# Attention and token mixer on one core: weight rows in contiguous eights, row-tiled transposes, and a transfer order from a queue model

## The chip, the cores and the metric

One core of one Trainium2 chip. The metric is device time in microseconds (us) of one execution; a profile's span is some 1.8 us shorter, since it runs from the first to the last instruction. TensorE (PE; its weight loads are PEld), VectorE (DVE), ScalarE (ACT), GpSimd (POOL) and SyncE (SP, which issues most DMAs) run side by side. "Clock" is the mean share of TensorE's full clock that the throttle granted.

## The reference

```python
scores = scale * (q @ k^T)          # 8 batches, 16 query heads over 4 key heads, 384 tokens, head 64
x = softmax(scores) @ v             # put together to [8, 384, 1024]
wq, wk = x @ w_q, x @ w_k           # both [1024, 64]
mixed = (scale * wq @ wk^T) @ x     # token mixing, no softmax
out = relu(mixed) @ w_out           # [1024, 1024]
```

Inputs and output are float32; the kernel computes in bf16 with float32 accumulation.

## The kernel before

The program is one long static list of instructions. A small scheduler in the generator keeps a clock for each engine, books a duration for every step and picks the next step for TensorE; its guesses fix the order, not the times on the chip. Four PSUM banks are shared by everything that is not a score. The parts that matter:

```python
def attend(b, g, u):                      # 12 matmuls of 65 columns, then the normalisation
    ...                                   # cut: ps = one of four banks
    nc.vector.reciprocal(out=rcp, in_=avv[:, :, D])
    nc.vector.tensor_tensor(out=xnats[b][:, c, h0:h0 + G, :], in0=avv[:, :, :D],
                            in1=rcp.to_broadcast([P, G, D]), op=ALU.mult)
    bank_free[at] = on("dve", 665, pe(370))      # what the scheduler books for it

def x_tr(b, c):                           # x transposed on TensorE: 8 blocks of 128x128 into one bank
    for dc in range(DC):
        nc.tensor.transpose(out=ps[:, dc, :], in_=xn[:, c, dc * P:(dc + 1) * P], identity=ident)
    nc.vector.tensor_copy(out=xTs[b][:, :, c, :], in_=ps)

def x_by_dma(b, c):                       # other chunks of x are transposed by DMA
    return b > 0 and c < C - 1
...                                       # cut: order of the first transfers
load(0); load(1)                          # k, q, v of batches 0 and 1
# w_q, w_k, then w_out: row c*128 + p on partition p
nc.sync.dma_start(out=wld[:, dc:dc + 2, :],
                  in_=moe_w_out[dc * P:(dc + 2) * P, :].rearrange("(c p) n -> p c n", p=P))
# load(2) follows when batch 1's scores begin, so behind w_out in the queue
```

`keep_busy` issues dummy matmuls (on a tile `idle`) where the scheduler sees TensorE wait, meant to hold its clock up (in the profile before, after 2.87 us without a matmul, the granted clock was 0.50 from 45 to 50 us).

The softmax here doesn't subtract the row's maximum and nothing guards it: scores larger than these inputs give would overflow.

Of the kernel before, what the change touches and what calls it, by code (L numbers as in the profile page):

```python
# [15 lines left out]
def kernel(  # L16
# [17 lines left out]

    nc = tc.nc
# [14 lines left out]
    NWIDE = 0  # L50
    NB = 4
    NPT = 9
    EAGER = 1
    DMA_TR = 5500
# [24 lines left out]
    clk = {"pe": 0.0, "dve": 0.0, "act": 0.0}  # L79
    mode = ["full"]  # L80
    wide_ps = [psG.tile([P, 2, NH], F32, name=f"wide{i}") for i in range(NWIDE)]
    bank_ps = [psG.tile([P, NH], F32, name=f"bank{i}") for i in range(NB)]
    wide_free = [0.0] * NWIDE
# [16 lines left out]

    def when(*keys):
        return max(ready.get(key, INF) for key in keys)
# [4 lines left out]

    def wide():
        return min((f, i) for i, f in enumerate(wide_free))
# [12 lines left out]
    def load(b):  # L122
        kraw = raw_p.tile([P, Hkv, C, D], F32, name="kraw")
        vraw = raw_p.tile([P, Hkv, C, D], F32, name="vraw")
        qraw = raw_p.tile([P, Hq, C, D], F32, name="qraw")
        raws[b] = (kraw, vraw, qraw)

        def ld(dst, src, a, z, c0=0, c1=C):
            nc.sync.dma_start(out=dst[:, a:z, c0:c1],  # L129
                              in_=src[b, a:z].rearrange("h (p c) d -> p h c d", p=P)[:, :, c0:c1])  # L130

        half = Hq // KP
        if b == 0:
            ld(kraw, k, 0, 2)
            ld(qraw, q, 0, half, 0, 1)
            ld(qraw, q, 0, half, 1, C)
            ld(vraw, v, 0, 2)
            ld(kraw, k, 2, 4)
            ld(qraw, q, half, Hq)
            ld(vraw, v, 2, 4)  # L140
        else:
            ld(kraw, k, 0, 4)
            ld(qraw, q, 0, half)
            ld(qraw, q, half, Hq)
            ld(vraw, v, 0, 4)
# [5 lines left out]
    def cast_k(b, kp, eng):  # L151
        for u in range(2):
            eng.tensor_copy(out=nats[b][0][:, kp, :, u, :], in_=raws[b][0][:, 2 * kp + u])  # L153

    def cast_q(b, kp, eng):
        for u in range(2):
            h0 = (2 * kp + u) * G
            eng.tensor_copy(out=nats[b][1][:, :, kp, :, u, :].rearrange("p c i d -> p i c d"),  # L158
                            in_=raws[b][2][:, h0:h0 + G])

# [4 lines left out]
    def cast_v(b, kp, eng):  # L165
        eng.tensor_copy(out=vexts[b % 3][:, 2 * kp:2 * kp + 2, :, :D],
                        in_=raws[b][1][:, 2 * kp:2 * kp + 2])

# [17 lines left out]
    def tr_dma(b, part):  # L186
        kb, qb = nats[b]
        KT, QT = trs[b]
        if part == 0:
            nc.sync.dma_start_transpose(out=KT, in_=kb.rearrange("p a c u d -> p (a c u d)"))  # L190
            for kp in range(KP):
                ready["K", b, kp] = clk["pe"] + DMA_TR
        else:
            c, n = part - 1, KP * G
            nc.sync.dma_start_transpose(out=QT[:, c * n:(c + 1) * n, :],
                                        in_=qb[:, c].rearrange("p a i u d -> p (a i u d)"))
            for kp in range(KP):
                ready["Q", b, kp, c] = clk["pe"] + DMA_TR

    def tr_k(b, kp0, kp1):  # L200
        kb, _ = nats[b]
        KT, _ = trs[b]
        _, i = bank()
        ps = bank_ps[i].bitcast(BF16).rearrange("p (n t) -> p n t", n=8)
        n = 0
        for kp in range(kp0, kp1):
            for c in range(C):
                nc.tensor.transpose(out=ps[:, n, :], in_=kb[:, kp, c].rearrange("p u d -> p (u d)"),
                                    identity=ident)
                n += 1  # L210
        nc.vector.tensor_copy(out=KT[:, kp0 * C:kp1 * C, :], in_=ps[:, :n, :])
        done = bank_free[i] = on("dve", 360 if n == C else 560, pe(56 * n))
# [3 lines left out]
    def tr_q(b, blocks):  # L216
# [3 lines left out]
        _, i = bank()  # L220
        ps = bank_ps[i].bitcast(BF16).rearrange("p (n t) -> p n t", n=8)
        for n, (c, kp) in enumerate(blocks):
            for j in range(G):
                nc.tensor.transpose(out=ps[:, n * G + j, :],
                                    in_=qb[:, c, kp, j].rearrange("p u d -> p (u d)"), identity=ident)
        end = pe(56 * G * len(blocks))
        if len(blocks) == 2 and blocks[1][0] == blocks[0][0]:
            t0 = (blocks[0][0] * KP + blocks[0][1]) * G
            nc.vector.tensor_copy(out=QT[:, t0:t0 + 2 * G, :], in_=ps)
            done = on("dve", 690, end)  # L230
        else:
            for n, (c, kp) in enumerate(blocks):
                t0 = (c * KP + kp) * G
                nc.vector.tensor_copy(out=QT[:, t0:t0 + G, :], in_=ps[:, n * G:(n + 1) * G, :])
                done = on("dve", 420, end)
        bank_free[i] = done
# [34 lines left out]
    def attend(b, g, u):  # L271
# [3 lines left out]
        if g == 0 and u == 0:  # L275
            xnats[b] = x_p.tile([P, C, Hq, D], BF16, name="xnat", bufs=3)
# [3 lines left out]
        for i in range(G):  # L280
            for kc in range(C):
# [7 lines left out]
        nc.vector.tensor_tensor(out=xnats[b][:, c, h0:h0 + G, :], in0=avv[:, :, :D],  # L289
                                in1=rcp.to_broadcast([P, G, D]), op=ALU.mult)  # L290
# [9 lines left out]
    def x_by_dma(b, c):  # L300
        return b > 0 and c < C - 1
# [8 lines left out]
    def x_tr_dma(b, c):  # L310
        x_open(b)
        xn = xnats[b].rearrange("p c h d -> p c (h d)")
        nc.sync.dma_start_transpose(out=xTs[b][:, :, c, :], in_=xn[:, c, :])
        ready["T", b, c] = when(("X", b, c, 0), ("X", b, c, 1)) + DMA_TR

    def x_tr(b, c):
        x_open(b)
        xn = xnats[b].rearrange("p c h d -> p c (h d)")
        _, i = bank()
        ps = bank_ps[i].bitcast(BF16).rearrange("p (n t) -> p n t", n=DC)  # L320
        for dc in range(DC):
            nc.tensor.transpose(out=ps[:, dc, :], in_=xn[:, c, dc * P:(dc + 1) * P], identity=ident)  # L322
        nc.vector.tensor_copy(out=xTs[b][:, :, c, :], in_=ps)  # L323
        ready["T", b, c] = bank_free[i] = on("dve", 690, pe(450))
# [19 lines left out]
    def wk_tr(b):  # L344
        wT, _ = wqs[b]
        _, i = bank()
        ps = bank_ps[i].bitcast(BF16).rearrange("p (n t) -> p n t", n=8)
        for c in range(C):
            nc.tensor.transpose(out=ps[:, c, :], in_=wT[:, c * P:(c + 1) * P], identity=ident)  # L349
        wkN = small_p.tile([P, C, Dh], BF16, name="wkN")  # L350
        nc.vector.tensor_copy(out=wkN, in_=ps[:, :C, Dh:2 * Dh])
        wkNs[b] = wkN
        ready["N", b] = bank_free[i] = on("dve", 250, pe(165))

    def mix_c(b):
        wkN = wkNs[b]
        xn = xnats[b].rearrange("p c h d -> p c (h d)")
# [37 lines left out]
    def po():  # L395
# [29 lines left out]
        if half == 1 and not last:  # L425
            nc.sync.dma_start(out=dst, in_=osb)

# [5 lines left out]
    def after_s(b, s):  # L433

        n = b + 1
        if b == 0 or n >= B:
            return
        if s == 0:
            load(n)
        elif s == 5:  # L440
            cast(n)
            start_tr(n)
        elif s in (9, 11, 13, 15):
            tr_dma(n, (s - 9) // 2)
# [17 lines left out]

    def cand_a():
# [3 lines left out]
        return max(when(*[("P", b, C * g + kc) for kc in range(C)]), ready["V", b], bank()[0])  # L467
# [12 lines left out]
    def chain_open(b):  # L480
        todo = []
        for c in range(C):
            if not x_by_dma(b, c):
                todo.append((lambda c=c: when(("X", b, c, 0), ("X", b, c, 1)), lambda c=c: x_tr(b, c), 1))
        todo.append((lambda: max(when(*[("T", b, c) for c in range(C)]), ready["Wt"]), lambda: wqk(b), 1))
        todo.append((lambda: when(("W", b)), lambda: wk_tr(b), 1))
# [13 lines left out]
    def cand_po():  # L500
# [4 lines left out]
        if i is None:  # L505
            t = max(t, when(("M", b, DCS[-1])), bank()[0])
        return t

    def step():
# [15 lines left out]
        for b in sorted(chains):  # L525
# [5 lines left out]
            if todo[0][-1] == "tiled" and pair is not None and pair < now + 1200:  # L531
# [8 lines left out]
        if not cands:  # L540
            return False
        ok = [x for x in cands if x[0] <= now]
# [4 lines left out]
        if go is None:  # L547
# [3 lines left out]
            for b in sorted(chains):  # L551
                todo = chains[b]
                if todo and todo[0][-1] == "tiled" and cand_chain(b) <= clk["pe"] + 20:
                    todo.pop(0)[1]()
                    break
# [3 lines left out]

# [9 lines left out]
    nc.sync.dma_start(out=wqkld[:, :, 0, :], in_=moe_w_q.rearrange("(c p) h -> p c h", p=P))  # L569
    nc.sync.dma_start(out=wqkld[:, :, 1, :], in_=moe_w_k.rearrange("(c p) h -> p c h", p=P))  # L570
    wld = wld_p.tile([P, DC, Dm], F32, name="wld")
    for dc in range(0, DC, 2):
        nc.sync.dma_start(out=wld[:, dc:dc + 2, :],
                          in_=moe_w_out[dc * P:(dc + 2) * P, :].rearrange("(c p) n -> p c n", p=P))
# [5 lines left out]
    clk["pe"] = clk["dve"] = clk["act"] = 4000.0  # L580
    tr_k(0, 0, 1)
    cast_qc(0, 0, 0, 0, nc.vector.tensor_copy)
    cast_qc(0, 0, 0, 1, nc.scalar.copy)
    keep_busy(900)
    clk["pe"] = clk["dve"] = 5200.0
# [11 lines left out]
    nc.gpsimd.tensor_copy(out=wqk_sb[:, :, Dh:], in_=wqkld[:, :, 1, :])  # L597
    for dc in range(DC):
        nc.gpsimd.tensor_copy(out=wout_sb[:, dc, :], in_=wld[:, dc, :])  # L599

    for b in range(B):
        ready["V", b] = 0.0
    ready["V", 0] = 11000.0
    ready["Wt"], ready["Wo"] = 24000.0, 30000.0
    prep += [
        (lambda: 8600.0, lambda: tr_q(0, [(1, 0), (2, 0)])),
        (lambda: 12500.0, lambda: tr_k(0, 1, 2)),
        (lambda: 13500.0, lambda: tr_q(0, [(0, 1), (1, 1)])),
        (lambda: 13500.0, lambda: tr_q(0, [(2, 1)])),
        (lambda: 21000.0, lambda: tr_k(1, 0, 2)),  # L610
        (lambda: 22000.0, lambda: tr_q(1, [(0, 0), (0, 1)])),
        (lambda: 22000.0, lambda: tr_q(1, [(1, 0), (1, 1)])),
        (lambda: 22000.0, lambda: tr_q(1, [(2, 0), (2, 1)])),
    ]
    prep = [(lambda at=at: max(at(), bank()[0]), lambda go=go: (prep.pop(0), go())) for at, go in prep]
# [33 lines left out]
```

## Time and profile before

| | before |
|---|---|
| time, at first | 224.09 us median of 3 (223.12 to 225.83) |
| TensorE busy | 95% of a span of 224.3 us |
| VectorE / ScalarE busy | 65% / 63% |
| x normalisation (L289) | 96 x 425 ns |
| the profiled execution | 226.12 us, clock 0.985, slower than every timed run (the record marks its state as slow) |

The prediction below shows the lines that carry this. How to read them: TensorE is at work nearly all the time and after about 50 us never waits, so the end is set by how much TensorE work is left then; a group's "idle before" names what its engine waited for, and its mean is the length of one record, not the pace (L322's transposes are 220 ns long and start 56 ns apart).

### The profile page before, as it was taken

How to read it: one execution, taken by the hardware profiler on the slowest of the kernel's cores; microseconds unless marked ns; L12 is line 12 of the kernel's file. 1: busy time of each engine (PE TensorE's matmuls, PEld its weight loads, DVE VectorE, ACT ScalarE, POOL GpSimd, SP SyncE). 2: the span in 40 equal slices, each digit the busy share in tenths (PEclk: the TensorE clock that was granted, in tenths of full speed). 3: DMA queues.
4: the chain of work that ended last, by engine and by line, in shares of the span. 5: the costliest groups of instructions: out<-in, count | busy, mean ns of one | idle time of the engine just before them, and what ended most of it. 6: DMA issues, size and time to landing. Idle time of an engine off the chain costs nothing.

```text
span 224.3 us, 5470 instructions
## 1 busy us (share of the span) xinstructions
PE 214.2 (95%) x2217; PEld 113.6 (51%) x2244; DVE 145.2 (65%) x365; ACT 140.6 (63%) x146; POOL 52.1 (23%) x97
## 2 busy tenths in 40 slices
PE   8999999589999999999999999999999999999993
PEld 5666665245545545454555546554555553434441
DVE  2355786834697758865887648874679569576332
ACT  3599998747788778887887887887888600000000
POOL 1385678406300540045016100620000000000000
PEclk9999999959999999999999999999999999999999
DMA  6996999999399979999999998989224422242424
GB/s 174 324 327 170 410 386 325 136 237 323 65 183 215 335 166 187 222 338 216 223 229 342 154 213 260 281 205 154 99 91 53 143 93 93 93 190 93 180 101 187
DMA packets 71688, 46.09 MB, mean 205 GB/s; under 512 B 42736, under 2 KB 67568, under 8 KB 71664
## 3 DMA queue, kind: packets, MB, share of 16 engines
q1 hardware_dynamic: 71520, 45.62, 77.6%
q8 instruction: 17, 0.28, 0.5%
q10 hardware_dynamic: 144, 0.13, 0.2%
q14 instruction: 7, 0.06, 0.1%
HBM read 23.59 MB, written 12.58 MB: 161 GB/s over the span
## 4 chain that ended last, share of the span: by engine, by line
PE 74%; DMA 14%; DVE 3%; SPq 3%; POOL 3%; issue 1%; DVEq 0%
PE bank L408 37%; PE bank L282 13%; PE sc L259 12%; DMA qraw<-in_q_dram 12%; PE bank L331 4%; SPq L129 3%; PE bank L384 3%; PE bank L362 2%; DMA QT<-qb 2%; PE bank L322 1%; POOL qb L158 1%; DVE osb L421 1%; PE bank L349 1%; DVE msb L389 1%; POOL wqk_sb L596 1%
## 5 line engine op out<-in xcount | busy, mean ns | idle before, releaser
L263 ACT ACTIVATE pt<-sc 128x1024 bf16<-128x1024 f32 x144 | 138.9, 1023 | 34.6 <-PE sc L259 34.4
L408 PE MATMUL bank<-wout_sb,msb 128*128 128x512 bf16 x357 | 91.7, 382 | 1.3 <-issue 0.5
L408 PEld LDWEIGHTS <-msb 128*128 128x128 bf16 x384 | 33.8, 98 | 42.4 <-issue 13.7
L259 PE MATMUL sc<-QT,KT 64*128 64x512 bf16 x288 | 47.5, 387 | 3.1 <-DMA QT<-qb 2.9
L282 PEld LDWEIGHTS <-pt 128*128 128x128 bf16 x1152 | 41.9, 98 | 15.8 <-issue 9.9
L282 PE MATMUL bank<-vext,pt 128*128 128x65 bf16 x1152 | 46.9, 195 | 0.4 <-DVE osb L421 0.2
L421 DVE COPY osb<-bank 128x512 f32<-128x512 f32 (+1 forms) x49 | 33.1, 677 | 21.7 <-PE bank L408 20.5
L289 DVE TENSOR_TENSOR xnat<-bank,rcp 128x256 bf16<-128x256 f32 x96 | 40.8, 425 | 3.3
L389 DVE TENSOR_SCALAR msb<-bank 128x384 bf16<-128x384 f32 x64 | 32.5, 551 | 9.5 <-PE bank L384 9.0
L287 DVE RECIPROCAL rcp<-bank 128x4 f32<-128x4 f32 x96 | 16.9, 176 | 17.6 <-PE bank L282 16.7
L158 POOL CAST qb<-qraw 128x768 bf16<-128x768 f32 x30 | 24.0, 827 | 17.4 <-DMA qraw<-in_q_dram 15.1
L153 POOL CAST kb<-kraw 128x192 bf16<-128x192 f32 x30 | 9.2, 347 | 67.3 <-DMA kraw<-in_k_dram 67.3
L259 PEld LDWEIGHTS <-KT 64*128 64x128 bf16 x288 | 12.4, 94 | 24.1 <-issue 17.2
L117 PE MATMUL bank<-idle 128*128 128x256 bf16 x80 | 14.8, 324 | 1.0 <-DVE idle L562 1.0
L331 PE MATMUL bank<-xT,wqk_sb 128*128 128x384 bf16 x64 | 11.7, 327 | 0.0
L117 PEld LDWEIGHTS <-idle 128*128 128x128 bf16 x80 | 7.9, 114 | 6.6 <-issue 4.0
L384 PE MATMUL bank<-wT,Csb 64*128 64x384 bf16 x32 | 10.6, 332 | 0.4 <-DVE rcp L287 0.3
L384 PE MATMUL bank<-wq,Csb 64*128 64x384 bf16 x32 | 10.6, 332 | 0.0
L599 POOL CAST wout_sb<-wld 128x1024 bf16<-128x1024 f32 x8 | 8.1, 1040 | 4.1 <-DMA wld<-in_moe_w_out_dram 4.1
L366 DVE CAST Csb<-bank 128x512 bf16<-128x512 f32 x8 | 5.5, 688 | 5.2 <-PE bank L362 5.2
L337 DVE CAST wT<-bank 128x384 bf16<-128x384 f32 x8 | 4.5, 558 | 6.7 <-PE bank L331 6.7
L323 DVE COPY xT<-bank 128x1024 bf16<-128x1024 bf16 x10 | 6.9, 688 | 2.5 <-PE bank L322 2.5
(33 smaller groups left out, 70.1 us busy)
## 6 DMA issues: line engine op xcount, KB each, us to landing
out_dram<-osb SPq DMA_DIRECT2D x23, 512.0 KB, 3.1
qraw<-in_q_dram SPq DMA_DIRECT2D x15, 768.0 KB, 7.4
wld<-in_moe_w_out_dram SPq DMA_DIRECT2D x4, 1024.0 KB, 9.5
kraw<-in_k_dram SPq DMA_DIRECT2D x7, 384.0 KB, 4.3
vraw<-in_v_dram SPq DMA_DIRECT2D x7, 384.0 KB, 8.9
qraw<-in_q_dram SPq DMA_DIRECT2D x1, 512.0 KB, 5.3
kraw<-in_k_dram SPq DMA_DIRECT2D x2, 192.0 KB, 3.7
vraw<-in_v_dram SPq DMA_DIRECT2D x2, 192.0 KB, 6.3
```

Source lines behind the costliest of these rows:

```text
L117: nc.tensor.matmul(out=bank_ps[i][:, :256], lhsT=idle[:, :P], rhs=idle, start=True, stop=True)
L158: eng.tensor_copy(out=nats[b][1][:, :, kp, :, u, :].rearrange("p c i d -> p i c d"), in_=raws[b][2][:, h0:h0 + G])
L259: nc.tensor.matmul(out=ps[:, u, :], lhsT=KT[lo:hi, kp * C + kc, :], rhs=QT[lo:hi, t0:t0 + G, :].rearrange("k i p -> k (i p)"), start=True, ...
L263: nc.scalar.activation(out=pt.rearrange("k u i p -> k u (i p)"), in_=ps, func=AF.Exp, scale=attn_scale)
L282: nc.tensor.matmul(out=ps[:, i * DE:i * DE + D + 1], lhsT=tiles[kc][:, u, i, :], rhs=vext[:, 2 * kp + u, kc, :D + 1], start=(kc == 0), sto ...
L287: nc.vector.reciprocal(out=rcp, in_=avv[:, :, D])
L289: nc.vector.tensor_tensor(out=xnats[b][:, c, h0:h0 + G, :], in0=avv[:, :, :D], in1=rcp.to_broadcast([P, G, D]), op=ALU.mult)
L331: nc.tensor.matmul(out=ps, lhsT=wqk_sb[:, dc, :], rhs=xT[:, dc].rearrange("d c p -> d (c p)"), start=(dc == 0), stop=(dc == DC - 1))
L384: nc.tensor.matmul(out=bank_ps[i][:, :S], lhsT=Csb[lo:hi, j * P:(j + 1) * P], rhs=w[lo:hi, :], start=True, stop=True)
L389: nc.vector.tensor_scalar_max(out=msb[:, dc, :], in0=bank_ps[i][:, :S], scalar1=0.0)
L408: nc.tensor.matmul(out=ps, lhsT=msbs[b][:, dc, c * P:(c + 1) * P], rhs=wout_sb[:, dc, half * NH:(half + 1) * NH], start=(nd == 0), stop=(n ...
L421: nc.vector.tensor_copy(out=osb[:, n0:n1], in_=ps[:, n0 - half * NH:n1 - half * NH])
```

## The change

Its intent: load the weights in longer contiguous pieces, halve the array time of the transposes that stay on TensorE and place them beside score bursts (which run in the same 64-row tiling mode), and get batch 2's inputs in ahead of w_out. The core of the diff (cut: the queue model's bookkeeping, q and k transposes, which are tiled in the same way, the start):

```diff
-            xnats[b] = x_p.tile([P, C, Hq, D], BF16, name="xnat", bufs=3)
+            xnats[b] = x_p.tile([P, C, DC, P], BF16, name="xnat", bufs=3)
...
-        nc.vector.tensor_tensor(out=xnats[b][:, c, h0:h0 + G, :], in0=avv[:, :, :D],
-                                in1=rcp.to_broadcast([P, G, D]), op=ALU.mult)
+        r = P // Hq
+        nc.vector.tensor_tensor(
+            out=xnats[b][:, c].rearrange("p e (h r) -> p h r e", r=r)[:, h0:h0 + G],
+            in0=avv[:, :, :D].rearrange("p i (r e) -> p i r e", r=r),
+            in1=rcp.unsqueeze(2).unsqueeze(3).to_broadcast([P, G, r, DC]), op=ALU.mult)
...
+    def half_trs(srcs):                        # two 64-row halves side by side, a bank for each
+        for j, src in enumerate(srcs):
+            for half in range(2):
+                lo, hi = half * H, (half + 1) * H
+                nc.tensor.transpose(out=outs[half][:, j, :], in_=src[lo:hi], identity=ident[lo:hi, lo:hi])
...
-        return b > 0 and c < C - 1
+        return b > XPE and c < C - 1           # XPE = 1: batch 1's x is transposed on TensorE too
...
-    nc.sync.dma_start(out=wqkld[:, :, 0, :], in_=moe_w_q.rearrange("(c p) h -> p c h", p=P))
+    nc.sync.dma_start(out=wqkld[:, :, 0, :], in_=moe_w_q.rearrange("(p c) h -> p c h", p=P))
+    load(2)                                    # ahead of w_out
+    wout_rows = moe_w_out.rearrange("(p c) n -> p c n", p=P)
```

With row 8p + e of a weight on partition p, column 8p + e of x has to lie at place p of block e. So the inner loop of the normalisation, over e, reads eight neighbours in PSUM and writes eight bf16 that lie 256 bytes apart.

## The prediction

> **What bounds the kernel now.** I read the page from the top: busy shares, the forty slices, then the chain of work that ended last, then that chain in order of time, then the stretches where it changes character.
>
> ```profile
> PE 214.2 (95%) x2217; PEld 113.6 (51%) x2244; DVE 145.2 (65%) x365; ACT 140.6 (63%) x146; POOL 52.1 (23%) x97
> ...
> PEclk9999999959999999999999999999999999999999
> ...
> GB/s 174 324 327 170 410 386 325 136 237 323 65 183 215 335 166 187 222 338 216 223 229 342 154 213 260 281 205 154 99 91 53 143 93 93 93 190 93 180 101 187
> ...
> PE 74%; DMA 14%; DVE 3%; SPq 3%; POOL 3%; issue 1%; DVEq 0%
> ```
>
> TensorE is 95% busy and carries 74% of the chain, so TensorE work is time, with one exception: the clock row has a 5 in its ninth slice (44.9 to 50.5 us), and 14% of the chain is DMA. The chain in order of time says what that DMA is:
>
> ```profile
> 24.88 14.96 DMA qraw<-in_q_dram
> 39.90 1.60 POOL qb L158 x2
> 41.53 3.79 DMA QT<-qb
> 45.45 0.61 PE sc L259 x2
> ```
>
> Batch 2's q load is asked for at about 24.9 us and lands at 39.9, is cast on GpSimd, transposed by DMA, and only then can batch 2's scores start at 45.45. The load waits because the 4 MB of w_out stand ahead of it in the same queue. What TensorE does around it, by stretch (columns: busy time and count of PE, PEld, DVE, ACT, POOL; then granted clock, DMA share, GB/s):
>
> ```profile
> 30.00:42.60 12.60, 12.47 (x167) 6.97 (x165) 9.93 (x28) 11.64 (x14) 10.18 (x15) 1.00 1.18 285
> 42.60:51.30 8.70, 5.77 (x40) 2.73 (x41) 3.68 (x11) 4.02 (x5) 0.52 (x2) 0.61 1.04 228
> 51.30:177.00 125.70, 123.56 (x1428) 65.53 (x1449) 89.95 (x236) 100.84 (x104) 26.07 (x49) 1.00 0.86 204
> 177.00:221.00 44.00, 43.44 (x234) 19.11 (x236) 25.97 (x47) 1.02 (x1) 0.00 (x0) 1.00 0.33 133
> ```
>
> Up to 42.6 us ScalarE is the pace (11.64 of 12.6 us busy) and TensorE fills its waits with dummy matmuls (L117). From 42.6 to 51.3 TensorE runs 40 matmuls in 8.7 us at a mean clock of 0.61. From 51.3 to 221 it has no dummy matmul at all (the eighty L117 instructions end before) and the last 44 us are nearly only the output projection L408: TensorE is always supplied, so the end is 51.3 us plus the TensorE work then left. Any useful work moved ahead of 51.3, or removed after it, comes off the end one for one. The groups that the change touches:
>
> ```profile
> L322 PE MATMUL bank<-ident,xnat 128*128 128x128 bf16 x80 | 6.1, 220 | 0.0
> L224 PE MATMUL bank<-ident,qb 128*128 128x128 bf16 x48 | 4.1, 228 | 0.0
> L349 PE MATMUL bank<-ident,wT 128*128 128x128 bf16 x24 | 2.6, 219 | 0.2 <-DVE wT L337 0.2
> L289 DVE TENSOR_TENSOR xnat<-bank,rcp 128x256 bf16<-128x256 f32 x96 | 40.8, 425 | 3.3
> L599 POOL CAST wout_sb<-wld 128x1024 bf16<-128x1024 f32 x8 | 8.1, 1040 | 4.1 <-DMA wld<-in_moe_w_out_dram 4.1
> ```
>
> [...]I use start-to-start times from the timeline instead: 56 ns for a 128-column transpose (eight start within 0.45 us), 216 ns for a 512-column matmul, about 30 ns for L282.
>
> [...]2.87 us without a matmul before 45.45, then a clock of 0.50 in 45 to 50 us. [...]the two 64-row matmuls of L384 start together (39.51), and a score burst that follows a full-array matmul starts some 95 ns later than the columns alone explain (32 cases after L408, mean 95 ns).[...]
>
> **The change part by part.**
>
> *Transfer order.* load(2) goes ahead of w_out; batch 1's x transposes move from DMA to TensorE, so no DMA transpose waiting for xnat (3.46 us of SyncE at 35.18) stands ahead of batch 2's transposes. A batch of q, k, v is 2.36 MB; at the 325 GB/s row that is 7.3 us. w_out is 4.19 MB; at some 400 GB/s, 10.4 us. With loads 0 and 1 done at about 17 us and the small weights at 18.5 to 20, load(2) ends at 26 to 27.5 and w_out at 36.5 to 38. Casts of q then end about 31 (GpSimd takes 3.2 us for both halves), so the transposes wait behind w_out in the ring, not for data: KT at about 39 to 40, the first QT at 41 to 42, the others every 1.8 us. Batch 1's scores run out at 42.6. I expect no long stall there and therefore no half clock.
>
> *Price of that order.* w_out is ready later: the last pair of casts (2.02 us) ends at 36.1 now, and at about 40 to 41.5 after. That costs nothing before, since the first projection starts at 49.98; and the change also lets batch 0's projection start after its first mixed pair instead of its last. So TensorE has projection work from about 41 us.
>
> *Worth.* In 42.6 to 51.3 the old kernel did three score pairs (3 x 0.22), 24 L282 (24 x 0.03), one mixed pair (0.16), three L408 (3 x 0.216): 2.2 us at full clock, and eight mode switches x 0.095 = 0.8: 3.0 us of work in 8.7. Filled, the stretch gives **5.7 us**. Two fillers at 40.08 and such idle before 42.6 give perhaps 0.3 more.
>
> *Row-tiled transposes.* Two 64-row halves of 64 moving columns side by side: [...]29 ns per source block if the pair starts within 3 ns as the score pairs do (estimate from those starts). An x transpose of eight blocks goes from 0.45 to 0.24 us. Only work after about 42 us counts: before, 7 (one for each of batches 1 to 7) x 0.45 = 3.15; after, 3 + 6 = 9 x 0.24 = 2.1: 1.0 saved though two more are done. wk's transposes: 7 x (0.17 - 0.09) = 0.5. Next to a score burst they need no switch of their own; some at the end, without bursts, pay 0.19 each: minus 0.3. Sum **1.2 us**. The q and k transposes of batches 0 and 1 lie in the ScalarE-paced part: nothing.
>
> *Added on VectorE.* Each transposed bank is evicted as two halves: 420 x 2 against 690 ns, 0.15 x 12 = 1.8 us; L289 writes bf16 with a 256-byte step. VectorE is 72% busy from 51.3 to 177, so neither is on the path if the step costs little. Each x transpose wants two of four banks at once. For bank waits I put **+0.8 us**.
>
> *Weights in contiguous eights.* Rows of 8 KB for w_out instead of 4 KB, 2 KB source runs for w_q and w_k instead of 256 bytes[...].
>
> Sum: 224.1 - 5.7 - 0.3 - 1.2 + 0.8 = 217.7; rounded toward the smoother start, **217.5 us**.
>
> **Rivals.** (a) *The wait moves rather than goes.* Batch 2's transposes land behind w_out at 44 or later, or w_out's casts end so late that TensorE has dummies alone from 41 to 44. For: the DMA queue is near full to 50 us, and DMA transposes move only some 200 GB/s at 43 to 48 us. Against: TensorE then has the one while the other is late; both must be late to idle it. One late wait without a clock drop: 220; with the clock drop: 222 to 224. (b) *VectorE becomes the bound.* If the stepped write of L289 costs 250 ns more, 96 x 0.25 = 24 us are added, from 145 to 171 of 218 us; banks come free late and TensorE waits: 221 to 227. Against: [...]425 ns is 256 elements[...], and the write may hide in it. (c) *The half transposes are no cheaper*, because [...]they bring their own mode switches: the 1.2 us turn into minus 1: 219.5. (d) *The chain of batch 1 gets too long*: nine tiled steps, one after each burst of 2.4 us, delay its projection to about 66 us while batch 0's 48 matmuls (10.4 us) must last that long; dummies would appear at 60 to 66 us: 219 to 220.
>
> **Range and chances.** 217.5 rests on one large term (5.7) that is either mostly had or mostly lost, and small ones of 1 to 2 us. All terms favourable: 214.5. Rival (a) in its mild form or (c) plus (d): 221.5. Two per cent faster is 219.6 us. I give (a) in a form that takes more than half about 15%, (b) 8%, small losses that add up to 2 us another 10%: faster 0.70, same 0.26, slower 0.04.
>
> **What would show it.** Right: no 5 in the clock row; batch 2's first scores at 42 to 43.5 us with KT and QT not in the chain for more than 1 us; L408 starting at 40 to 43; the dummies still about 80 or fewer and none after 45; the x transposes (96 blocks as 192 half matmuls) at about 29 ns per pair; L289 still near 425 ns; the pure projection tail shorter. Wrong: a PE wait on QT or wout_sb above 2 us, a clock under 0.9 after 10 us, L289 above 500 ns with VectorE over 75% busy, or "95 ns" gaps around single transposes. If L289 has grown and TensorE waits on VectorE's evictions, rival (b) is the cause.

## The result, and the profile after

| | time, us | ratio to before |
|---|---|---|
| before, same rounds | 223.61 (222.86 to 225.83), 4 runs | |
| after | 267.08 (265.82 to 268.21), 4 runs | 1.192 (1.182 to 1.203) |

A ratio is the mean time of one kernel's fast runs over that of the other's fast runs in the same rounds, so it is not quite the ratio of the medians. The result is correct, and 43 us slower. The page of the changed kernel, in the order in which I read that of before: busy shares, the slices of TensorE, VectorE and the clock, the chain that ended last.

```profile
PE 221.8 (84%) x2383; PEld 111.7 (42%) x2413; DVE 219.3 (83%) x391; ACT 141.4 (54%) x146; POOL 52.1 (20%) x97
...
PE   7977787878987698788898798888878898899994
...
DVE  2797998988888988999799998998899989968432
...
PEclk9999899779999999999999999999999999999999
...
DVE 53%; PE 39%; issue 5%; DMA 1%; SPq 0%; DVEq 0%
```

VectorE has 219 us of work instead of 145, fills eight or nine tenths of most slices, and has taken the chain from TensorE. The clock row has an 8 and two 7s: at a mean clock of 0.981 some 5 us of TensorE time are lost that way ((1 - 0.981) x 264.1, an estimate), so a small part of the 43 us can be clock. The groups name the one operation behind it (busy us and mean ns stand after the bar):

```profile
L312 DVE TENSOR_TENSOR xnat<-bank,rcp 128x256 bf16<-128x256 f32 x96 | 124.5, 1297 | 4.2
L430 PE MATMUL bank<-wout_sb,msb 128*128 128x512 bf16 x354 | 90.9, 383 | 10.1 <-DVE rcp L309 4.7
```

The same 96 operations on the same shapes take 1297 instead of 425 ns: 83.7 us more. What that does to TensorE, its timeline first, then VectorE's at the same time:

```profile
51.22 0.32 PE L406 MATMUL bank<-wT,Csb 64*128 64x384 bf16 x1
51.45 0.32 PE L406 MATMUL bank<-wq,Csb 64*128 64x384 bf16 x1
52.86 0.32 PE L406 MATMUL bank<-wT,Csb 64*128 64x384 bf16 x1 [1.10 <-DVE rcp L309]
54.22 0.32 PE L406 MATMUL bank<-wq,Csb 64*128 64x384 bf16 x1 [1.03 <-DVE xnat L312]
```

```profile
51.51 1.30 DVE L312 TENSOR_TENSOR xnat<-bank,rcp 128x256 bf16<-128x256 f32 x1
52.44 0.38 DVE L309 RECIPROCAL rcp<-bank 128x4 f32<-128x4 f32 x1
52.87 1.29 DVE L312 TENSOR_TENSOR xnat<-bank,rcp 128x256 bf16<-128x256 f32 x1
53.79 2.14 DVE L411 TENSOR_SCALAR msb<-bank 128x384 bf16<-128x384 f32 x4
```

The two halves of a mixed pair are meant to run side by side in two row tiles. In the kernel before they started within 10 ns of each other (39.51 and 39.51 in its timeline); here the second pair waits, each half for a bank that VectorE has still to empty, and its halves run 1.4 us apart (those of the first pair 0.23). Three further effects were as predicted or harmless: ScalarE's and GpSimd's work is unchanged (141.4 us against 140.6, and 52.1 in both), q, k and v land in about the same time (q in 7.6 us from the issue, 7.4 before), and w_out is cast by 41.4 us, before the first projection at 55.52.

### The profile page after: what moved, and what is told of

Same layout as the page of the kernel before. It is cut to its first block, busy times and chain, and to the rows that moved or that the text cites. A ratio compares the mean times of both kernels' runs of the same rounds, so it can differ in the third digit from the quotient of the medians.

```text
span 264.1 us, 5827 instructions
## 1 busy us (share of the span) xinstructions
PE 221.8 (84%) x2383; PEld 111.7 (42%) x2413; DVE 219.3 (83%) x391; ACT 141.4 (54%) x146; POOL 52.1 (20%) x97
## 4 chain that ended last, share of the span: by engine, by line
DVE 53%; PE 39%; issue 5%; DMA 1%; SPq 0%; DVEq 0%
DVE xnat L312 33%; PE bank L430 21%; DVE msb L411 6%; PE sc L281 6%; DVE osb L443 5%; PE bank L304 5%; DVE rcp L309 3%; PE bank L126 2%; PE bank L384 2%; PE bank L352 1%; DVE wq L360 1%; DVE Csb L388 1%; DVE wT L358 1%; DVE xT L235 1%; PE bank L229 1%
## 5 line engine op out<-in xcount | busy, mean ns | idle before, releaser
L312 DVE TENSOR_TENSOR xnat<-bank,rcp 128x256 bf16<-128x256 f32 x96 | 124.5, 1297 | 4.2
L304 PE MATMUL bank<-vext,pt 128*128 128x65 bf16 x1152 | 48.7, 195 | 7.2 <-DVE msb L411 2.0
L281 PE MATMUL sc<-QT,KT 64*128 64x512 bf16 x288 | 48.5, 394 | 0.2
L443 DVE COPY osb<-bank 128x512 f32<-128x512 f32 (+1 forms) x49 | 35.1, 718 | 12.0 <-PE bank L430 11.8
L411 DVE TENSOR_SCALAR msb<-bank 128x384 bf16<-128x384 f32 x64 | 35.7, 599 | 2.5 <-PE bank L406 2.2
L309 DVE RECIPROCAL rcp<-bank 128x4 f32<-128x4 f32 x96 | 25.1, 261 | 5.4 <-PE bank L304 5.0
L281 PEld LDWEIGHTS <-KT 64*128 64x128 bf16 x288 | 10.5, 94 | 21.1 <-issue 18.6
L126 PE MATMUL bank<-idle 128*128 128x256 bf16 x77 | 13.1, 303 | 3.6 <-DVE rcp L309 2.0
L235 DVE COPY xT<-bank 128x512 bf16<-128x512 bf16 x24 | 10.1, 467 | 2.3 <-PE bank L229 2.3
L229 PE MATMUL bank<-ident,xnat 64*128 64x64 bf16 x192 | 5.5, 190 | 4.9 <-DVE xnat L312 3.2
L642 POOL CAST wout_sb<-wld 128x1024 bf16<-128x1024 f32 x8 | 8.1, 1040 | 2.6 <-DMA wld<-in_moe_w_out_dram 2.6
```

The source lines that it names most:

```text
L126: nc.tensor.matmul(out=bank_ps[i][:, :256], lhsT=idle[:, :P], rhs=idle, start=True, stop=True)
L281: nc.tensor.matmul(out=ps[:, u, :], lhsT=KT[lo:hi, kp * C + kc, :], rhs=QT[lo:hi, t0:t0 + G, :].rearrange("k i p -> k (i p)"), start=True, ...
L304: nc.tensor.matmul(out=ps[:, i * DE:i * DE + D + 1], lhsT=tiles[kc][:, u, i, :], rhs=vext[:, 2 * kp + u, kc, :D + 1], start=(kc == 0), sto ...
L312: nc.vector.tensor_tensor(out=xnats[b][:, c].rearrange("p e (h r) -> p h r e", r=r)[:, h0:h0 + G], in0=avv[:, :, :D].rearrange("p i (r e) ...
L411: nc.vector.tensor_scalar_max(out=msb[:, dc, :], in0=bank_ps[i][:, :S], scalar1=0.0)
L443: nc.vector.tensor_copy(out=osb[:, n0:n1], in_=ps[:, n0 - half * NH:n1 - half * NH])
```

## The experiments

Thirteen runs. S stands for "the stepped write is the cause", T and D for its rivals; C, in the second profile of before, is a theory of its own and is explained there.

### Undoing the contiguous eights, or doing them alone

The changed kernel with straight rows:

```diff
-            out=xnats[b][:, c].rearrange("p e (h r) -> p h r e", r=r)[:, h0:h0 + G], ...
+            out=xnats[b].rearrange("p c e r -> p c (e r)")[:, c, h0 * D:(h0 + G) * D]..., in0=avv[:, :, :D],
+            in1=rcp.to_broadcast([P, G, D]), op=ALU.mult)
-    ... moe_w_q.rearrange("(p c) h -> p c h", p=P)      # w_k and w_out likewise
+    ... moe_w_q.rearrange("(c p) h -> p c h", p=P)
```

> The changed kernel with the contiguous eights undone: w_q, w_k and w_out rows on partitions as before, x written straight. Theory S (the stepped bf16 write of the x normalisation, 1297 instead of 425 ns, 96 times, made VectorE the bound and is the whole loss): the x normalisation back to 425 ns and the time at 217 to 219 us, as the rest of the prediction has it. Rival T (the row-tiled transposes with their double banks, or the new order, cost too): 224 us or more though the operation is short again.

Measured: 221.15 us (219.10 to 221.97, 4 runs), ratio 0.991 (0.984 to 0.998), the operation at 425 ns. The loss is gone. The median missed my 217 to 219 by 2 us; one run of the four did reach 219.10. The runs on the order and on the start, below, bear on that.

The kernel before with the permuted write and the permuted weight rows, nothing else:

> The kernel before with the contiguous eights alone (weight rows, x columns permuted), old transposes and old order. Theory S: the x normalisation at about 1300 ns and 260 to 272 us, near the changed kernel. Rival T: at most 240 us, since most of the loss would be the rest of the change.

Measured: 267.39 us, ratio 1.200 (1.191 to 1.210). Its group line:

```profile
L290 DVE TENSOR_TENSOR xnat<-bank,rcp 128x256 bf16<-128x256 f32 x96 | 124.6, 1298 | 4.4
```

Taken together: the contiguous eights make the whole loss, with or without the rest of the change.

### The same layout, the loops turned

```diff
-            out=xnats[b][:, c].rearrange("p e (h r) -> p h r e", r=r)[:, h0:h0 + G],
-            in0=avv[:, :, :D].rearrange("p i (r e) -> p i r e", r=r),
-            in1=rcp.unsqueeze(2).unsqueeze(3).to_broadcast([P, G, r, DC]), op=ALU.mult)
+            out=xnats[b][:, c].rearrange("p e (h r) -> p h e r", r=r)[:, h0:h0 + G],
+            in0=avv[:, :, :D].rearrange("p i (r e) -> p i e r", r=r),
+            in1=rcp.unsqueeze(2).unsqueeze(3).to_broadcast([P, G, DC, r]), op=ALU.mult)
```

> The changed kernel with only the loop order inside the x normalisation turned: runs of eight adjacent bf16 written, PSUM read with a 32-byte step. If the step of the write is what costs (theory S): 425 to 500 ns and 217 to 221 us. If the short inner loop of eight and the third free dimension cost (rival D): still about 1300 ns and 264 us or more. If a stepped PSUM read costs as much as a stepped write: above 800 ns.

Measured: 220.94 us (219.13 to 221.16), ratio 0.990 (0.984 to 0.996). Every byte lands where it did in the changed kernel and the weights keep their eights; only the order within the instruction differs: eight neighbours are written, and the step is on the PSUM read. The operation is back at 425 ns. So neither the layout nor the third loop costs anything, only the order in which the bf16 are written. Beside the straight-row kernel (0.991) it also shows that the longer weight pieces are worth nothing that these rounds resolve.

### The disputed cost by itself

Behind the end of the kernel before, eight operations of each kind on a scratch tile (wrong nowhere: the output is already written), for example:

```diff
+    for _ in range(8):
+        nc.vector.tensor_tensor(out=t_four, in0=av4, in1=one, op=ALU.mult)   # bf16, step of 8 bytes
```

> The kernel before, and after its end a row of VectorE and ScalarE operations of 128 x 256 elements alone, eight of each: writes with steps of 2, 4, 8, 16, 32 bytes in bf16, 8, 16, 32 bytes in fp32, the change's own pattern, the turned one, a stepped read with a dense write, copies with the same write, ScalarE the same. Theory S[...]: near 425 ns up to a step of 4 bytes, growing with the step and flat at about 1300 ns from 16 bytes on; fp32 with 16 bytes the same. Rival D: the steps cost nothing and only the pattern with three free dimensions is slow.

Its clock is 0.857 over a span of 310.5 us, of which the added tail, without a matmul, is some 90; I put the low mean down to that tail. In the order of the lines below: bf16 written straight (L641), with steps of 4, 8, 16 and 32 bytes (L643 to L649); fp32 with steps of 8, 16 and 32 bytes (L651 to L655); the change's pattern (L657) and the turned one (L659); a stepped read with a dense write (L661); the change's pattern as a copy from PSUM (L663) and from SBUF (L665); ScalarE straight (L667) and in the change's pattern (L669).

```profile
L641 DVE TENSOR_TENSOR wld<-bank,ones 128x256 bf16<-128x256 f32 x8 | 3.4, 424 | 0.4
L643 DVE TENSOR_TENSOR wld<-bank,ones 128x256 bf16<-128x256 f32 x8 | 3.5, 442 | 0.2
L645 DVE TENSOR_TENSOR wld<-bank,ones 128x256 bf16<-128x256 f32 x8 | 5.8, 723 | 0.2
L647 DVE TENSOR_TENSOR wld<-bank,ones 128x256 bf16<-128x256 f32 x8 | 10.3, 1294 | 0.2
L649 DVE TENSOR_TENSOR wld<-bank,ones 128x256 bf16<-128x256 f32 x8 | 10.0, 1252 | 0.2
L651 DVE TENSOR_TENSOR wld<-bank,ones 128x256 f32<-128x256 f32 x8 | 3.6, 447 | 0.2
L653 DVE TENSOR_TENSOR wld<-bank,ones 128x256 f32<-128x256 f32 x8 | 4.8, 604 | 0.2
L655 DVE TENSOR_TENSOR wld<-bank,ones 128x256 f32<-128x256 f32 x8 | 4.9, 615 | 0.2
L657 DVE TENSOR_TENSOR wqkld<-bank,ones 128x256 bf16<-128x256 f32 x8 | 10.4, 1295 | 0.2
L659 DVE TENSOR_TENSOR wqkld<-bank,ones 128x256 bf16<-128x256 f32 x8 | 3.4, 424 | 0.3
L661 DVE TENSOR_TENSOR wld<-bank,ones 128x256 bf16<-128x256 f32 x8 | 3.4, 423 | 0.2
L663 DVE CAST wqkld<-bank 128x256 bf16<-128x256 f32 x8 | 10.4, 1294 | 0.2
L665 DVE COPY wqkld<-wld 128x256 bf16<-128x256 bf16 x8 | 5.9, 736 | 0.3
L667 ACT CAST wqkld<-bank 128x256 bf16<-128x256 f32 x8 | 3.0, 373 | 118.8 <-DVE wqkld L663 118.6
L669 ACT CAST wqkld<-bank 128x256 bf16<-128x256 f32 x8 | 10.4, 1295 | 3.1 <-DVE wqkld L665 2.8
```

For bf16 the cost grows with the step (442 ns at 4 bytes, 723 at 8, 1294 at 16) and is flat from 16 bytes on: the change's 256 bytes cost what 16 do (1295). It is a cost of the write and not of the read (a stepped read with a dense write takes 423 ns, the straight operation 424), of both operations from PSUM that I tried (1295 and 1294), and of ScalarE as much (1295 ns against 373 straight). The source matters too: fed from bf16 in SBUF, the same write takes 736 ns (L665). No straight copy from SBUF stands beside it, so what it would cost unstepped is not known. My guess that fp32 with 16 bytes would be as dear was wrong: 604 ns. And since the cost is flat from 16 bytes on, I counted what each write touches in groups of 16 bytes ("lines" in the next expectation): 442, 723 and 1294 ns for 64, 128 and 256 of them fitted a flat charge of some 4.45 ns for each, an estimate:

> The kernel before, and after its end VectorE operations alone, eight of each, 128 x 256: single bf16 with steps of 32 and 64 bytes, runs of 2, 4, 8 and 16 adjacent bf16 with a gap to the next 64-byte group, runs of 2 and 4 fp32 the same. If the cost is one charge of 4.45 ns for every 16-byte line written in bf16 (as the first steps fit: 442, 723, 1294 ns for 64, 128, 256 lines): runs of two 128 lines and 725 ns, runs of four 64 lines and 440, eight 424. If what costs is the lone 2-byte element whatever its line: runs of two already 424.

Single bf16 with steps of 32 and 64 bytes (L642, L644), runs of two and of eight neighbours (L646, L650), runs of two fp32 (L654):

```profile
L642 DVE TENSOR_TENSOR wld<-bank,ones 128x256 bf16<-128x256 f32 x8 | 9.8, 1225 | 0.4
L644 DVE TENSOR_TENSOR wld<-bank,ones 128x256 bf16<-128x256 f32 x8 | 10.1, 1268 | 0.3
...
L646 DVE TENSOR_TENSOR wld<-bank,ones 128x256 bf16<-128x256 f32 x8 | 3.4, 424 | 0.3
...
L650 DVE TENSOR_TENSOR wld<-bank,ones 128x256 bf16<-128x256 f32 x8 | 3.4, 423 | 0.2
...
L654 DVE TENSOR_TENSOR wld<-bank,ones 128x256 f32<-128x256 f32 x8 | 3.4, 423 | 0.2
```

Two neighbouring bf16 are enough to make the write as cheap as the straight one (424 ns in both), though 128 groups of 16 bytes are touched. The flat charge for a group is refuted: what is dear is a bf16 written alone, without its neighbour next in order (1225 and 1268 ns). Why a lone one with a step of 4 bytes is nearly free (442 ns) is not explained by that, and stays open.

### How the cost of one operation becomes the cost of the kernel

83.7 us of operation time cost 46 us of kernel time against the turned kernel (267.08 less 220.94). Half a dose, in the same layout with a right result:

```diff
+        if u == 1:
+            dst, src = dst.rearrange("p h r e -> p h e r"), src.rearrange("p i r e -> p i e r")
```

> The changed kernel, 48 of its 96 x normalisations with the stepped write and 48 with the turned order (same layout, right result). Added VectorE time 48 x 0.87 = 42 us instead of 84. Linear theory (each long operation delays the path by about half its excess, wherever it falls): halfway between 220.9 and 267, 242 to 246 us. Threshold theory (VectorE has slack of some 38 us, = 84 added less 46 of lost time, and only what exceeds it costs): 224 to 231 us.

Measured: 241.87 us, ratio 1.084 (1.076 to 1.091). Over the turned kernel's 0.990 that is 0.094 for half of the long operations, and 0.202 for all. That is near the linear theory (the time is just under its 242 to 246 us) and refutes the threshold of 38 us; a free allowance of a few us is not excluded by one half dose. VectorE was 76% busy (80 to 84% between 50 and 200 us), TensorE 89%: the loss begins long before VectorE is full. In this profile TensorE waited for VectorE some 17 us in all.

Two more runs asked whether VectorE's throughput or the order of the instructions makes that. First the booking, with 1000 ns in place of 665 (the true 1535 gave an order that deadlocks in the simulator):

```diff
-        bank_free[at] = on("dve", 665, pe(370))
+        bank_free[at] = on("dve", 1000.0, pe(370))
```

> The changed kernel, the generator's booking for the evicting step of the attention raised from 665 to 1000 ns (1535 would be the true one and gives an order that deadlocks in the simulator), so that the instruction order fits the long operation better. If the wrong order makes the loss: 255 us or less. If VectorE's throughput does: within 2 per cent of 267.

Measured: 259.32 us, ratio 1.160 (1.152 to 1.167) in place of 1.192: some 7 us less (0.033 of 223) than with the order as it was. Stretches 50 to 100, 100 to 150 and 150 to 200 us, the changed kernel first, then this one (columns as in the prediction; VectorE's busy time is the fourth number):

```profile
50.00:100.00 50.00, 40.38 (x476) 20.37 (x481) 43.85 (x79) 29.18 (x30) 8.05 (x15) 0.97 0.49 124
100.00:150.00 50.00, 41.84 (x464) 20.44 (x469) 45.27 (x77) 32.90 (x34) 10.62 (x20) 1.00 0.75 200
150.00:200.00 50.00, 42.71 (x459) 20.95 (x465) 45.90 (x79) 30.08 (x32) 5.34 (x11) 1.00 0.64 152
```

```profile
50.00:100.00 50.00, 41.95 (x521) 21.62 (x527) 47.93 (x84) 36.42 (x38) 7.82 (x14) 1.00 0.69 145
100.00:150.00 50.00, 41.87 (x493) 21.57 (x499) 47.45 (x84) 33.70 (x36) 10.67 (x20) 1.00 0.76 188
150.00:200.00 50.00, 44.81 (x502) 22.58 (x510) 47.48 (x81) 34.24 (x36) 5.32 (x10) 1.00 0.56 140
```

Then less VectorE work at the old order, 23 projection evictions given to ScalarE:

```diff
-            nc.vector.tensor_copy(out=osb[:, n0:n1], ...)
+            (nc.vector.tensor_copy if half or last else nc.scalar.copy)(out=osb[:, n0:n1], ...)
```

> The changed kernel in the same order, with 23 of the 48 projection evictions moved from VectorE to ScalarE: some 17 us of VectorE's 219 go, ScalarE (54 per cent busy) takes them. If VectorE's throughput is the bound: 267 less 9 to 17 us, 250 to 258. If the order or the length of the single operation is the bound: 264 us or more.

Measured: 263.75 us, ratio 1.180 (1.172 to 1.187). VectorE lost 13.7 us of work (219.3 to 205.6), the kernel some 3 us, and the interval overlaps that of the changed kernel. The test is weaker than I meant it: the evictions left on VectorE fell from 35.1 to 18.2 us, but only some 10 us of that lie before 210 us, where nearly all the long operations are; the rest is in the projection tail. Neither rival alone gives what was seen. The changed kernel leaves VectorE 88 to 92% busy in its body, the better booking 95 to 96%, so part of the loss (at least some 7 us of 46, since 1000 ns is still booked too low) is an order planned for a 425 ns operation; and once the order is better VectorE is nearly full. That its throughput is all of the rest is argued, not shown: I did not separate them further.

### What the rest of the change is worth

First a second profile of the kernel before, unchanged:

> The kernel before, unchanged, for a second profile. Its timed runs of the last call list a clock of 1.000 at 221.9 to 222.7 us and of 0.992 at 223.8 to 224.4, and the profile on record was 226.1 us at 0.985. Theory C (the half clock around 45 us is a matter of luck, and the record's profile showed a bad case): a profile at a clock of 0.99 to 1.00, 2.9 us or less without matmuls at 42 to 46 us, and little or no slice under 9 in the clock row. Rival: the same 5 in the clock row as on record, so that the gap of 2 to 4 us between the runs has another cause.

It took 223.27 us at a clock of 0.999. Its clock row, the stretches 40 to 45 and 45 to 50 us, and the first score of batch 2:

```profile
PEclk9999999999999999999999999999999999999999
```

```profile
40.00:45.00 5.00, 2.20 (x36) 1.16 (x34) 3.72 (x10) 3.26 (x4) 1.94 (x4) 1.00 1.16 166
45.00:50.00 5.00, 4.95 (x70) 2.88 (x72) 2.29 (x8) 3.98 (x4) 0.00 (x0) 1.00 1.01 234
```

```profile
44.99 0.39 PE L259 MATMUL sc<-QT,KT 64*128 64x512 bf16 x2 [2.69 <-DMA QT<-qb]
```

The stall is there (2.69 us), the half clock is not: where the profile had 38 matmuls at a clock of 0.50 in 45 to 50 us, this one has 70 at 1.00. The timed runs of before fall into two kinds. Of the 36 whose clock is listed, 19 took 221.9 to 222.9 us at 0.998 to 1.000 and 17 took 223.8 to 225.2 us at 0.991 or 0.992. The row-tiled run below was profiled at 0.992 and shows what that is: a 7 in the ninth slice of its clock row (44.2 to 49.7 us), with 2.1 us of waiting on QT. Going by their clocks alone, 17 of the 36 have one too. The profile at 0.985 was worse than both kinds, and my prediction took it for the rule.

The order alone, with straight rows and full-array transposes (the diff is the straight-row one plus the old transposes):

> Straight rows and the old full-array transposes, so the new transfer order (with batch 1's x transposes on TensorE and the new start) alone. If the order carries what is left of the gain: 219.5 to 221.5 us, ratio 0.985 to 0.995, with no wait on QT or qraw above 1 us in the chain. If the row-tiled transposes carry it: 222.5 to 224.

Measured: 219.91 us (219.44 to 221.50, 6 runs), ratio 0.986 (0.981 to 0.992), about 3.1 us (0.0139 of 222.5). In its timeline TensorE waits at most 0.23 us at a time between 38 and 52 us, the first projection starts at 46.07, and the stall on QT is gone from the chain. This run also carries the new start, so the 3.1 us are not the order's alone. Its profile is of its slowest execution (221.50 us): there batch 1's last scores start at 41.96 us, in the second profile of before (223.27 us) at 41.74, so what comes after that point is some 2.0 us shorter. That much is the order; the rest lies in the start and in the half-clock runs that are in the mean of before.

The row-tiled transposes alone, on the kernel before:

> The kernel before with the row-tiled transposes alone. By the prediction's step (1.2 us saved): 221.3 us, ratio 0.995. By the rival (c), which the straight-row profile speaks for (190 to 260 ns lost at the switch behind each short row-tiled group, where it was 0 to 80 behind a full-array one): ratio 1.00 or above, 222.5 to 224.

Measured: 222.65 us, ratio 0.998 (0.992 to 1.003): not told apart from nothing, and the predicted 0.995 is inside the interval too. The mechanism is half there in the straight-row kernel's timeline beside the order-alone one's. A tiled x transpose behind a burst starts at 46.38 and the next group at 46.71, 0.33 us with the change from 64-row to full-array matmuls in it; a full-array one starts at 46.30 and the next group at 46.74, 0.44 us. The tiled one also follows the burst sooner (0.44 us from the burst's start, where a full-array group takes 0.54), which makes the 0.21 us predicted. But only five of the nine tiled x transposes after 42 us do this; behind the other four the next group comes after 0.56 us (at 48.87 with an issue wait of 0.16 in it), and nothing is gained. My expectation had read a loss of 190 to 260 ns behind every such group; it is there behind some.

The changed kernel with the turned loops and wk's transposes back on the full array:

> The changed kernel with the turned loop order (runs of eight written) and wk's transposes back on the full array: the eights, the order and the x tiles kept. Seven switches of about 190 ns go, seven times 80 ns of array time come back: 219.5 to 221.5 us, ratio 0.985 to 0.995, no measurable step from the kernel with wk tiled (0.9899), and faster than the kernel before.

Measured: 219.39 us (219.21 to 221.34, 6 runs), ratio 0.986 (0.980 to 0.992): faster than both kernels. Its runs, like those of the straight-row and turned kernels, fall in two groups, near 219.3 and near 221. The first 10 us show where they part. First the straight-row kernel of 219.10 us, then the turned one of 220.87:

```profile
5.25 0.83 PE L126 MATMUL bank<-idle 128*128 128x256 bf16 x6
6.01 0.61 PE L281 MATMUL sc<-QT,KT 64*128 64x512 bf16 x4
```

```profile
5.41 1.46 PE L126 MATMUL bank<-idle 128*128 128x256 bf16 x6
6.80 1.03 PE L281 MATMUL sc<-QT,KT 64*128 64x512 bf16 x4
```

Six dummies in 0.83 or in 1.46 us: the array runs at little more than half the pace in the second, though the granted clock is listed as 1.00 from 5 to 10 us in both. By batch 1's last scores, which start at 40.67 and 42.44 us, the whole difference of the two spans (217.3 and 219.1) is there. So I put three dummies in the pause of 0.6 us ahead of the first q transposes:

```diff
     tr_k(0, 0, 1)
+    keep_busy(3 * FILL + 80)
     clk["pe"] = 5000.0
```

> The version with the turned order and wk's transposes on the full array, plus three dummy matmuls in the wait for the first K copy. Its runs fell in two groups, 219.2 to 219.4 and 220.8 to 221.3, and one kernel's profile of each group shows the TensorE clock warm at about 4.2 us or only at about 9.4. If the pause of 0.64 us at 4.4 is what delays the clock: all runs at 219.0 to 219.6. If not: the two groups stay; median 219 to 221, faster than the kernel before either way.

Measured: 219.51 us (219.35 to 220.06, 6 runs), ratio 0.983 (0.979 to 0.988), against 223.76 for before in those rounds. All six runs lie within 0.7 us, the upper group did not appear; six runs are few for that (the kernel without the dummies had two of six in the upper group, so six low ones would come by chance about once in eleven times: (4/6)^6). It is the best version here: 1.7% less time than before and 17.5% less than the changed kernel (0.983 over 1.192).

## Why the prediction was wrong

**The step that failed** is "Added on VectorE": "L289 writes bf16 with a 256-byte step. VectorE is 72% busy from 51.3 to 177, so neither is on the path if the step costs little." I put it at nothing inside +0.8 us for bank waits. The runs showed 872 ns more for each of 96 operations, 83.7 us, and 46 us of kernel time. The sum had a term of zero where its largest term belonged.

**The rival was named and mis-sized.** Rival (b), VectorE becoming the bound, is what happened, and the sign that I gave for it (L289 above 500 ns, VectorE over 75%) is what the profile shows. I gave it 8% and sized it at 250 ns and 221 to 227 us. The argument against it has a number for the pace of the whole operation alone (425 ns for 256 elements); that the write hides in it has none. I set a large cost of the step aside although the trace before had no such instruction (but for a memset of 12 elements, L566), so that nothing measured bounded it. Absence from the trace was a reason to widen the range, not to drop the term. The terms gave 214.5 to 221.5, which left the case of a dear step out altogether.

**The slack.** I took a VectorE that is 72% busy to be off the path. The half dose, 0.094 of time for 42 us of added work, shows that TensorE is delayed while VectorE still has idle time. That the long operation does it by holding one of the four banks fits the waits in the timeline above, but no run tests it alone.

**Transfer order.** The mechanism was right: in the kernel before, GpSimd got batch 2's last q at 39.90 us, after w_out's last rows at 34.06; in the changed one, with the load ahead of w_out, at 28.21, and w_out's last rows at 39.37 (KT's transpose, issued behind w_out at 27.54, took 12.5 us to land, where the median of the six is 3.8). No stall on QT, no 5 in the clock row in the straight-row kernel, w_out's later arrival free. Batch 2's first scores came later than predicted, at 43.57 to 45.53 us in the three profiles without the stepped write (straight rows, turned loops, order alone), but TensorE had other work until then. The size was off: the term was 5.7 us, and the run of the order gives 3.1 us with the new start in it, some 2.0 without. About half of 5.7 was the half clock, which the second profile does not have (226.12 less 223.27 is 2.85). By their clocks the profiled run lost some 3.4 us that way ((1 - 0.985) x 224.3), a timed run at 0.992 some 1.8, and the others nothing (estimates): the sum started from the median of the timed runs and took off the whole loss of the profiled one.

**Row-tiled transposes.** 1.2 us predicted; 0.5 us measured with an interval from 1.7 faster to 0.6 slower. Unresolved in size, and small as said; four of nine gain nothing, as shown above. Rival (c), a loss from it, is not supported in sum; rivals (a) and (d) did not occur in the runs without the stepped write.

**Weights in contiguous eights.** No term of the sum: the turned kernel (0.990) against the straight-row one (0.991) agrees with no effect.

With the stepped write out of it, the turned kernel is 1.0% faster than before (2.2 us, 0.990 of 222.67) where the sum had 6.6 us. The order term (5.7 predicted, at most 3.1 measured) is the largest part of the difference that the runs show; the slow start, seen in its profile and by their times in three of its four runs, is another, some 1.8 us between the two profiles above.

## What to carry to other kernels

When a layout change turns an evicting write into lone 2-byte elements, look at the loop order before anything else: put the dimension that is contiguous in the destination innermost and the step on the PSUM read, where it cost nothing here (425 ns, against 1297 with the step on the write). A suspected cost without a number is a reason to measure, or to leave room for in the range; the same operation tripled in time here (425 to 1297 ns) with the same shapes on the profile line. And before a loss seen in one profile is booked as gain, compare that run's time and clock with the timed runs.

## What the runs showed of the hardware

- bf16 written alone, with 16 bytes or more from one to the next, took 1225 to 1298 ns for 128 x 256 elements from PSUM against 424 straight, some 3.4 ns more for each element of a partition ((1297 - 425) / 256, an estimate); ScalarE took 1295 against 373. One fp32 to 16 or 32 bytes took 604 and 615, half of the bf16. Two lone bf16 to 16 bytes (8-byte step) took 723 ns, while two neighbours with a gap behind them took 424.
- A stepped PSUM read with a dense write cost VectorE nothing (423 ns with a 32-byte step).
- A row-tiled score burst behind full-array matmuls starts some 95 ns later than their columns explain (an estimate from the starts in the trace before: three 512-column matmuls of 216 ns at 53.18 us, the burst at 53.93).
- The same kernel, the one before, had a gap of 2.87 us with a clock of 0.50 in 45 to 50 us in one execution, and a gap of 2.69 us with a clock of 1.00 there in another; so a single profile does not tell what a gap costs. By the clocks of the stretches around it (0.92, 0.50, 0.90 in 40 to 45, 45 to 50 and 50 to 55 us) the half clock of the first lasted some 6.8 us (44.2 to 51.0, an estimate); the row-tiled run, with 2.1 us of waiting on QT and a mean clock of 0.992, lost some 1.8 us to the clock ((1 - 0.992) x 220.8, an estimate), about half of what the first lost (3.4).
- The start of the kernel before, whose TensorE works on from 1.04 us without a pause, was still slow up to 5.90 us in its first profile: seven dummies start within 1.49 us from 4.41, 213 ns each; five at 9.06 took 112 each. Two kernels with the same opening instructions and a pause of 0.6 us in them differ: in the straight-row one nine dummies from 6.55 us took 1.16 us, in the turned one nine from 7.77 took 1.71.
